# A fused attention and two feed-forwards: the first feed-forward's sums in single PSUM banks, and the split of its result later in the step

## Chip, cores and metric

The kernel runs on 1 core of one Trainium2 chip. The metric is the device time of one execution in microseconds (us), the median of several runs. Engines are named as in the profile: PE is TensorE (PEld its weight loads), DVE is VectorE, ACT is ScalarE, POOL is GpSimd and SP is SyncE, which here only issues DMAs.

## What is computed

The reference chains three blocks. The attention masks its scores by hash buckets of queries and keys. Its output, 1536 tokens of 512 numbers, is the input of feed-forward A, whose output is the input of feed-forward B:

```
h = x @ w_in                                   # A: 512 -> 2048
P = a[0] + a[1]*h + a[2]*h*h + a[3]*h*h*h
Q = 1 + |b[0]|*|h| + |b[1]|*h*h
x2 = (P / (Q + 1e-6)) @ w_out                  # 2048 -> 512

p = sinkhorn(exp(x2 @ w_gate - max))           # B: 1536 tokens, 8 experts, 8 rounds
for e in range(8):
    out += p[:, e:e+1] * (relu(x2 @ w1[e]) @ w2[e])     # 512 -> 1024 -> 512
```

The weights of A arrive as 64-bit floats and are narrowed on the chip; those of B are 32-bit.

## The kernel before

**Products of halves.** Every large operand is split into a high part (fp32r) and a low part (what the high part misses). A product is three matmuls: high by high, high by low, low by high. The tile pairs are `xh`/`xl` for A's input, `gh`/`gl` for hidden activations, `x2h`/`x2l` for B's input, `wa` and `wb` for the weights of a feed-forward's first and second product.

**Feed-forward A in steps.** The hidden width of 2048 is cut into 4 quarters `qf` of 4 blocks of 128, the tokens into 3 tiles `tt` of 512. A pair (qf, tt) is a unit, and a unit has 4 steps, one for each block: 48 steps in all (`NS`), numbered s = 0 to 47 here. PE does in step s:

- `gemm1` (L346, called by `step_a`): 12 matmuls into a bank `h`, called h(s) below;
- `gemm2_a` (L396), from step 6 on: 12 matmuls of the unit that is complete by then, for one of 4 blocks of output rows, into `acca`. It is called g2(s) below. It reads the hidden activations of four earlier steps, the youngest of step s-3.

`acca` is one PSUM tile of two banks, and g2(s) writes bank `j % 2` of it. `sum_a` then adds this bank to the running sum `part` in SBUF (DVE, L407; for the first quarter a copy on ACT, L104 with the output `part`). In the last quarter the finished `part` is split into `x2h` (ACT, L104) and `x2l` (DVE, L107), which B's first product reads.

**Activation.** `activate_a` (L358 to 377) turns h(s) into `gh` and `gl`: ACT forms `tw`, `tq`, `tu` (L364 to 366), POOL a product (L367), DVE two (L368, L369). One step later ACT forms the reciprocal in a bank `tr` (L372 log, L373 exponential), DVE does three operations (L374, L375, L376), ACT writes `gh` (L104) and POOL `gl` (L101). Banks `h` and `tr` come from one set of 4 single banks (tag "b").

**Narrowing the weights.** `prep_weights` works in pieces: ACT takes absolute values (L165), POOL clips (L166), DVE assembles bits in four operations (L176 to L179) over a second two-bank tile `cvt`, POOL adds (L182), ACT writes the high part, POOL the low part. It happens in two of every three steps, from step 3 to step 37.

**What sets the order.** PSUM has 8 banks: 4 single ones under tag "b", and 2 tiles of two banks under tag "s". The latter serve the attention's scores, then `acca` and `cvt`, then B's accumulators `acc0` and `acc1`. In feed-forward A, and in the first 6 steps of B beside it (s = 48 to 53), the order on PE, ACT, DVE and POOL is the order in which the loop over s (L630 to 662) issues the work (`manual_schedule`). On DVE this is, in step s: L374, L375, L376 of step s-1; L368, L369 of step s; the four bit operations if there are any; L407. The lists `old_w`, `acting` and `narrowing` hold work of the step before; `summing` holds the sums whose split into halves is still to come, and `old_s` resumes them, ahead of all the others.

**Feed-forward B.** 8 experts by 3 token tiles by 8 blocks make 192 steps: 12 matmuls of the first product (`step_b`, L346) and 12 of the second (`gemm2_b`, L441), accumulated over the 8 blocks in the four banks of `acc0` and `acc1`. After the last block DVE adds the four banks, weighted, to `osum` (L454). Outside the hand-ordered loop a scheduler sets the order.

Of the kernel before, what the change touches and what calls it, by code (L numbers as in the profile page):

```python
# [13 lines left out]
F32 = mybir.dt.float32  # L14
# [8 lines left out]
PSUM = bass.MemoryType.PSUM  # L23
# [11 lines left out]
def kernel(  # L35
# [22 lines left out]
    P = 128  # L58
# [26 lines left out]
    ps = ctx.enter_context(tc.tile_pool(name="ps", bufs=4, space=PSUM))  # L85
# [2 lines left out]
        return ps.tile([P, 512], F32, tag="b", bufs=4, name=name)  # L88

    def two_banks(name):  # L90
        return ps.tile([P, 2, 512], F32, tag="s", bufs=2, name=name)

    def split(eng_hi, eng_lo, hi, lo, src):
        eng_hi(hi, src)
# [8 lines left out]
    def act_copy(o, src):  # L103
        act.activation(o, src, AF.Copy)  # L104

    def dve_lo(lo, src, hi):
        dve.tensor_tensor(lo, src, hi.bitcast(F32), ALU.subtract)  # L107


    qkv_pool_stack = ExitStack()  # L110
    ap = qkv_pool_stack.enter_context(tc.tile_pool(name="attn", bufs=2))
    heads = [(b, h) for b in range(B) for h in range(H)]
    loaded = {}

# [54 lines left out]
    def narrow_b(bits, c):  # L169


        ci = c.bitcast(I32)
        pc = c if cvt is None else cvt[:, 0]
        pi = pc.bitcast(I32)
        low, high = bits[:, :, 0], bits[:, :, 1]
        dve.tensor_scalar(pi, ci, 5, 2, ALU.logical_shift_left, ALU.logical_shift_right)  # L176
        dve.scalar_tensor_tensor(high, high, -0x40000000, pi, ALU.bitwise_and, ALU.bitwise_or)
        dve.tensor_scalar(pi, high, -0x800000, None, ALU.bitwise_and)  # L178
        dve.scalar_tensor_tensor(low.bitcast(F32), low.bitcast(U32), 2.0 ** -52, pc, ALU.mult, ALU.mult)  # L179
# [4 lines left out]
    def prep_weights(m, i):  # L184

        if i >= NW:
            return
        one = wide and i < NA_W
        c, j = (i, 0) if one else divmod(i - NA_W, 2) if wide else divmod(i, 2)
        if wide and not one:  # L190
            c += NA_W
        r = raws[m, c]
        t = wslots[(i % NSLOT) // 4].tile([P, 2, 512], F32R, tag=f"w{'ab'[m]}{i % NSLOT}", name="w" + "ab"[m])
        slots[m, i] = tuple(t[:, k].rearrange("p (c f) -> p c f", c=KC) if m == 0 else t[:, k] for k in range(2))
        if one:
            bits = (r.rearrange("p c f -> p (c f)") if m == 0 else r[:, 0]).rearrange("p (n t) -> p n t", t=2)
            n = narrow_a(bits)
            yield
            narrow_b(bits, n)
            yield  # L200
            narrow_c(bits, n)
            load_weights(m, c + 2)
            yield
            act_copy(t[:, 0], n)
            yield
            pool_lo(t[:, 1], n, t[:, 0])
            return
        if m == 0:
            split(pool_hi, pool_lo, t[:, 0].rearrange("p (c f) -> p c f", c=KC),
                  t[:, 1].rearrange("p (c f) -> p c f", c=KC), r[:, :, j * P:(j + 1) * P])  # L210
        else:
            split(pool_hi, pool_lo, t[:, 0], t[:, 1], r[:, j])
        if j == 1:
            load_weights(m, c + 2)
# [138 lines left out]


    units = [(qf, tt) for qf in range(NQ) for tt in range(TT)]
    ahid = {}

    def activate_a(hps, gh, gl):  # L358

# [21 lines left out]
    def step_a(n, f):  # L381
        qf, tt = units[n]
        gh, gl = ahid[n, f] = hidden()
        hps = gemm1(slots[0, qf * QF + f], xh[tt], xl[tt])
        return activate_a(hps, gh, gl)

    def gemm2_a(n, j):
        qf, tt = units[n]
        o = acca[:, j % 2]
        js = slice(j * P, (j + 1) * P)  # L390
        m = 0
        for f in range(QF):
            bh, bl = slots[1, qf * QF + f]
            gh, gl = ahid[n, f]
            for l, r in ((bh, gh), (bh, gl), (bl, gh)):
                pe.matmul(o, lhsT=l[:, js], rhs=r, start=m == 0, stop=m == 3 * QF - 1)  # L396
                m += 1

    def sum_a(n, j):

        qf, tt = units[n]
        o = acca[:, j % 2]
        if qf == 0:
            part[tt, j] = sums.tile([P, 512], F32, tag=f"sum{tt}{j}", name="part")
            act_copy(part[tt, j], o)
            return
        dve.tensor_tensor(part[tt, j], part[tt, j], o, ALU.add)  # L407
        if qf == NQ - 1:
            yield
            if j == 0:  # L410
                x2h[tt] = xpool.tile([P, KC, 512], F32R, tag="xh", name="x2h")
                x2l[tt] = xpool.tile([P, KC, 512], F32R, tag="xl", name="x2l")
            act_copy(x2h[tt][:, j], part[tt, j])
            dve_lo(x2l[tt][:, j], part[tt, j], x2h[tt][:, j])
# [3 lines left out]
    bhid, baccs = {}, {}  # L418

    def step_b(n):  # L420
        e, tt, f = steps[n]
        gh, gl = bhid[n] = hidden()
        hps = gemm1(slots[0, FF // P + e * EF + f], x2h[tt], x2l[tt])

        def activate():
            act.activation(gh, hps, AF.Relu)  # L426
            dve.scalar_tensor_tensor(gl, hps, 0.0, gh.bitcast(F32), ALU.max, ALU.subtract)  # L427
        return activate

    def gemm2_b(n):  # L430
        e, tt, f = steps[n]
        bh, bl = slots[1, FF // P + e * EF + f]
        gh, gl = bhid[n]
        if f == 0:
            baccs[tt] = (two_banks("acc0"), two_banks("acc1"))
        acc = baccs[tt]
        for j in range(4):
            o = acc[j // 2][:, j % 2]
            js = slice(j * P, (j + 1) * P)
            for m, (l, r) in enumerate(((gh, bh), (gh, bl), (gl, bh))):  # L440
                pe.matmul(o, lhsT=l[:, js], rhs=r, start=f == 0 and m == 0, stop=f == EF - 1 and m == 2)  # L441
        if f == EF - 1:
            pr = gate["p"]
            for j in range(4):
                o = acc[j // 2][:, j % 2]
                n_ = tt * 4 + j
                if e == 0:
                    osum[n_] = sums.tile([P, 512], F32, tag=f"sum{tt}{j}", name="osum")
                if (e, tt) == (0, 0):
                    act_copy(osum[n_], o)  # L450
                elif e == 0:
                    dve.tensor_scalar(osum[n_], o, pr[:, n_, 0:1], None, ALU.mult)
                else:
                    dve.scalar_tensor_tensor(osum[n_], o, pr[:, n_, e:e + 1], osum[n_], ALU.mult, ALU.add)  # L454
                if e == E - 1:
                    b, c = divmod(n_, C)
                    sp.dma_start(out.rearrange("(b p c) d -> b c p d", b=B, c=C)[b, c], osum[n_])
# [83 lines left out]
    prep_head_b(0)  # L541

    wprep = {NG - 13 + 3 * j: j for j in range(QF)}
    cvt = None
    for it in range(NG + VLAG):
        if it == CONST_AT:
            ca = const.tile([P, 4], F32, name="ca")
# [40 lines left out]
                list(prep_weights(m, wprep[it]))  # L588
    qkv_pool_stack.close()

    def ffn_pool(name, bufs):
        return ctx.enter_context(tc.tile_pool(name=name, bufs=bufs, reuse_waits="tile"))

    wslots[1] = ffn_pool("wslots1", 1)
    mp = ffn_pool("ffn", 2)
    sums = ffn_pool("sums", 1)

    acca, cvt = two_banks("acca"), two_banks("cvt")
    NU, NS, NB_ = len(units), len(units) * QF, len(steps)
    QS = TT * QF  # L600

# [19 lines left out]
    def go(gen):  # L621

        return next(gen, 0) is None
# [3 lines left out]
    narrowing, acting, summing = [], [], []  # L627
    with tc.manual_schedule(engines={mybir.EngineType.PE, mybir.EngineType.Activation, mybir.EngineType.DVE,
                                     mybir.EngineType.Pool}):
        for s in range(NS + QF + ALAG):  # L630
            n = s - NS
            if n < 0:
                new = step_a(*divmod(s, QF))
            else:
                new = step_b(n)
            u, j = divmod(s - ALAG - QF, QF)
            if 0 <= u < NU:
                gemm2_a(u, j)
            old_w = narrowing
            narrowing = [prep_weights(m, i) for m, i in preps.get(s, ())]  # L640
            narrowing = [w for w in narrowing if go(w)]
            old_s = [w for w in summing if go(w)]
            for w in old_w:
                go(w)
            for w in acting:
                go(w)
            if n < 0:
                go(new)
            else:
                new()  # L650
            for w in acting:
                go(w)
            for w in old_w:
                go(w), go(w)
            for w in narrowing:
                go(w)
            summing = []
            if 0 <= u < NU:
                w = sum_a(u, j)
                if go(w):  # L660
                    summing.append(w)
            acting = [new] if n < 0 else []
        assert not (summing and any(go(w) for w in summing)) and not narrowing
# [52 lines left out]
```

## Time and profile before

| | us |
|---|---|
| median of 3 runs | 1665.94 (1664.51 to 1666.65) |
| the profiled execution, its own time | 1664.14 |
| its span, first to last instruction | 1662.4 |
| PE busy | 1591.3 (96%) |
| DVE busy | 736.7 (44%) |
| POOL busy | 657.3 (40%) |
| ACT busy | 563.3 (34%) |

Some 1.7 us of the execution's own time lie outside the span. Busy shares are averages over three stages with different limits: the attention up to about 292 us, feed-forward A up to about 619 us, feed-forward B to the end. The page's 40 slices show it: DVE is busy for seven to nine tenths of each slice up to slice 14 (about 590 us) and for one tenth after it, while PE is at nine or more nearly everywhere.

### The profile page before, as it was taken

The page shows a single profiled execution, that of the slowest core. Times are in us where ns is not written, and L with a number is a line of the kernel's source. Part 1 is how long each engine was busy: PE and PEld are TensorE (multiplying, and loading weights), DVE is VectorE, ACT ScalarE, POOL GpSimd, SP SyncE. Part 2 cuts the span into 40 slices and gives each one's busy share as a digit, 9 for nine tenths or more (in the row PEclk, how much of TensorE's full clock was granted, in tenths as well). Part 3 has the DMA queues.
Part 4 walks back from the last instruction along what each step waited for, and adds up shares of the span by engine and source line. Part 5 has one row for each costly group of instructions (what it writes and reads, how often), then busy time and mean ns, then how long its engine had stood idle before and what let it go on. Part 6 is the DMA issues. An engine that isn't in the chain of part 4 may idle for free.

```text
span 1662.4 us, 19660 instructions
## 1 busy us (share of the span) xinstructions
PE 1591.3 (96%) x7683; PEld 1317.5 (79%) x7683; DVE 736.7 (44%) x1314; ACT 563.3 (34%) x1025; POOL 657.3 (40%) x696
## 2 busy tenths in 40 slices
PE   6999999798888999999999999999999999999998
PEld 5888888576666787888888888888888888888887
DVE  7999999788888742311111111111111111111112
ACT  4887888787676731111111111111111111111110
POOL 7688775677667650150051051042033024015000
PEclk8999999999999999999999999999999999999999
DMA  5232220022111110020020011011012002001001
GB/s 166 80 91 75 73 67 14 26 64 64 51 51 52 38 51 13 14 76 13 1 76 26 0 64 38 1 51 51 1 37 65 0 26 76 1 13 38 1 26 51
DMA packets 49389, 71.67 MB, mean 43 GB/s; under 512 B 4369, under 2 KB 35089, under 8 KB 49297
## 3 DMA queue, kind: packets, MB, share of 16 engines
q1 hardware_dynamic: 49296, 70.42, 14.0%
q8 instruction: 60, 0.98, 0.2%
q14 instruction: 33, 0.26, 0.0%
HBM read 59.79 MB, written 3.15 MB: 38 GB/s over the span
## 4 chain that ended last, share of the span: by engine, by line
PE 74%; DVE 13%; ACT 4%; POOL 4%; issue 3%; DMA 0%; DVEq 0%; POOLq 0%
PE h L346 33%; PE acc L441 31%; PE acca L396 3%; PE av L315 2%; PE pt L300 2%; POOL e L286 1%; DVE tq L374 1%; DVE tu L376 1%; DVE tr L375 1%; DVE e L278 1%; DVE tu L368 1%; DVE ptl L107 1%; DVE cvt L178 1%; DVE cvt L176 1%; DVE part L407 1%
## 5 line engine op out<-in xcount | busy, mean ns | idle before, releaser
L346 PE MATMUL h<-x2h,wa 128*128 128x512 f32 x1536 | 504.7, 390 | 0.0
L427 DVE SCALAR_TENSOR_TENSOR gl<-h,gh 128x512 fp32r<-128x512 f32 x192 | 132.7, 691 | 797.4 <-ACT gh L426 797.4
L441 PE MATMUL acc<-wb,gh 128*128 128x512 f32 x1536 | 474.4, 389 | 0.0
L426 ACT ACTIVATE gh<-h 128x512 fp32r<-128x512 f32 x192 | 114.8, 598 | 894.3 <-PE h L346 894.3
L346 PEld LDWEIGHTS h<-x2h,wa 128*128 128x128 f32 x1536 | 288.5, 188 | 60.1
L441 PEld LDWEIGHTS acc<-wb,gh 128*128 128x128 f32 x1536 | 288.0, 188 | 60.0
L441 PE MATMUL acc<-wb,gl 128*128 128x512 f32 x768 | 298.8, 389 | 0.0
L346 PE MATMUL h<-x2l,wa 128*128 128x512 f32 x768 | 298.8, 389 | 0.0
L98 POOL TENSOR_SCALAR wa<-ra 128x512 fp32r<-128x512 f32 x64 | 40.3, 630 | 533.5 <-PE h L346 533.4
L441 PEld LDWEIGHTS acc<-wb,gl 128*128 128x128 f32 x768 | 144.1, 188 | 29.9
L346 PEld LDWEIGHTS h<-x2l,wa 128*128 128x128 f32 x768 | 144.0, 188 | 29.6
L396 PE MATMUL acca<-gh,wb 128*128 128x512 f32 x384 | 129.8, 399 | 28.9 <-DVE part L407 21.7
L346 PE MATMUL h<-xh,wa 128*128 128x512 f32 x384 | 127.2, 393 | 6.9 <-DVE tu L376 6.9
L396 PEld LDWEIGHTS acca<-gh,wb 128*128 128x128 f32 x384 | 72.2, 188 | 55.2 <-DVE part L407 26.5
L107 DVE TENSOR_TENSOR ptl<-pt,pth 128x512 fp32r<-128x512 f32 x144 | 94.3, 680 | 15.3 <-ACT pth L104 14.5
L286 POOL TENSOR_SCALAR e<-e,rs 128x768 f32<-128x768 f32 x96 | 90.2, 951 | 24.2 <-DVE rs L284 14.6
L279 ACT ACTIVATE e<-e,nm 128x768 f32<-128x768 f32 x96 | 89.8, 935 | 8.5 <-DVE e L278 7.7
L278 DVE TENSOR_SCALAR_CACHE_REDUCE e<-s 128x768 f32<-128x768 f32 x96 | 90.8, 947 | 2.0 <-PE s L271 1.7
L300 PE MATMUL pt<-idr,e 128*128 128x128 f32 x576 | 82.5, 278 | 9.2 <-DVE ptl L107 4.0
L346 PEld LDWEIGHTS h<-xh,wa 128*128 128x128 f32 x384 | 72.5, 189 | 23.6 <-DVE tu L376 8.6
L101 POOL TENSOR_TENSOR wa<-ra,wa 128x512 fp32r<-128x512 f32 x64 | 84.0, 1313 | 5.3
L101 POOL TENSOR_TENSOR wb<-rb,wb 128x512 fp32r<-128x512 f32 x64 | 83.7, 1308 | 5.2
(149 smaller groups left out, 2027.2 us busy)
## 6 DMA issues: line engine op xcount, KB each, us to landing
ra<-in_moe_w_dram SPq DMA_DIRECT2D x32, 512.0 KB
rb<-in_moe_w_dram SPq DMA_DIRECT2D x32, 512.0 KB
ra<-in_moe_w_in_dram SPq DMA_DIRECT2D x16, 512.0 KB
rb<-in_moe_w_out_dram SPq DMA_DIRECT2D x16, 512.0 KB
qkv<-in_q_dram SPq DMA_DIRECT2D x16, 192.0 KB
qkv<-in_k_dram SPq DMA_DIRECT2D x16, 192.0 KB
qkv<-in_v_dram SPq DMA_DIRECT2D x16, 192.0 KB
a<-a SPq DMA_DIRECT2D x16, 192.0 KB
```

The lines of the kernel that those rows point to most:

```text
L98: pool.tensor_scalar(hi, src, 1.0, 0.0, ALU.mult, ALU.add)
L101: pool.tensor_tensor(lo, src, hi.bitcast(F32), ALU.subtract)
L107: dve.tensor_tensor(lo, src, hi.bitcast(F32), ALU.subtract)
L278: dve.tensor_scalar(e[j], s[:, 0:S], BIG, None, ALU.min, ALU.min, accum_out=nm)
L279: act.activation(e[j], e[j], AF.Exp, bias=nm, scale=-1.0, accum_out=rs[:, j:j + 1])
L286: pool.tensor_scalar(e[j], e[j], rs[:, j:j + 1], 0.0, ALU.mult, ALU.add)
L300: pe.transpose(pt[:, c, j * P:(j + 1) * P], e[j][:, cc * P:(cc + 1) * P], idf)
L346: pe.matmul(hps, lhsT=a[:, c], rhs=x[:, c], start=m == 0, stop=m == 3 * KC - 1)
L396: pe.matmul(o, lhsT=l[:, js], rhs=r, start=m == 0, stop=m == 3 * QF - 1)
L426: act.activation(gh, hps, AF.Relu)
L427: dve.scalar_tensor_tensor(gl, hps, 0.0, gh.bitcast(F32), ALU.max, ALU.subtract)
L441: pe.matmul(o, lhsT=l[:, js], rhs=r, start=f == 0 and m == 0, stop=f == EF - 1 and m == 2)
```

## The change

Two things change.

**Banks.** The two-bank tiles stay for the attention alone, in a pool of their own (`ps_s`) that is closed with it. The four banks then go to a pool `ps_f` with single-bank tiles: three in turn under tag "f" and one under tag "c". `gemm2_a` takes a new tile from "f" for each g2(s), which `sum_a` finds under `aacc`. `narrow_b` takes the bank "c" for its bits (named `bits` now). B's four accumulators are the three "f" banks and "c".

**Order.** The second half of `sum_a`, which writes `x2h` and `x2l`, moves from the head of the next step to behind the `gh`, `gl` and weight pieces of that step, ahead of the next sum.

```
@@ two_banks
-        return ps.tile([P, 2, 512], F32, tag="s", bufs=2, name=name)
+        return ps_s.tile([P, 2, 512], F32, tag="s", bufs=2, name=name)
@@ narrow_b
-        pc = c if cvt is None else cvt[:, 0]
+        pc = sum_bank(3, "bits") if bits_in_psum else c
@@ gemm2_a
-        o = acca[:, j % 2]
+        o = sum_bank(0, "acca")
+        aacc[n, j] = o
@@ sum_a
-        o = acca[:, j % 2]
+        o = aacc.pop((n, j))
@@ gemm2_b
-            baccs[tt] = (two_banks("acc0"), two_banks("acc1"))
+            baccs[tt] = [sum_bank(j, f"acc{j}") for j in range(4)]
...
-            o = acc[j // 2][:, j % 2]
+            o = acc[j]
@@ after the attention
-    acca, cvt = two_banks("acca"), two_banks("cvt")
+    ps_f = ffn_pool("ps_f", 1, space=PSUM)
+
+    def sum_bank(j, name):
+
+        return ps_f.tile([P, 512], F32, tag="f" if j < 3 else "c", bufs=3 if j < 3 else 1, name=name)
+
+    bits_in_psum = True
@@ the loop over s
             narrowing = [w for w in narrowing if go(w)]
-            old_s = [w for w in summing if go(w)]
             for w in old_w:
                 go(w)
...
             for w in old_w:
                 go(w), go(w)
+            old_s, summing = summing, []
+            for w in old_s:
+                go(w)
             for w in narrowing:
                 go(w)
-            summing = []
             if 0 <= u < NU:
```

**On PE**, in the second quarter of A. These are one h(s), and the first rows of the g2(s) behind it, with the semaphores that they wait for (DVE_49 counts what DVE has finished); before:

```order
L346 MATMUL h_5190<-xh_97,wa_4304 128x512
L346 MATMUL h_5190<-xl_100,wa_4304 128x512
L346 MATMUL h_5190<-xh_97,wa_4304 128x512 x2
L346 MATMUL h_5190<-xl_100,wa_4304 128x512
L346 MATMUL h_5190<-xh_97,wa_4304 128x512 x2
L346 MATMUL h_5190<-xl_100,wa_4304 128x512
L346 MATMUL h_5190<-xh_97,wa_4304 128x512 x2
L346 MATMUL h_5190<-xl_100,wa_4304 128x512
L346 MATMUL h_5190<-xh_97,wa_4304 128x512
L396 MATMUL acca_4157<-gh_4699,wb_4398 128x512 [waits DVE_49]
L396 MATMUL acca_4157<-gl_4700,wb_4398 128x512
```

The same place with the change (its line numbers are 1 and 2 higher):

```order
L347 MATMUL h_5222<-xh_100,wa_4310 128x512 [waits DVE_49]
L347 MATMUL h_5222<-xl_103,wa_4310 128x512
L347 MATMUL h_5222<-xh_100,wa_4310 128x512 x2
L347 MATMUL h_5222<-xl_103,wa_4310 128x512
L347 MATMUL h_5222<-xh_100,wa_4310 128x512 x2
L347 MATMUL h_5222<-xl_103,wa_4310 128x512
L347 MATMUL h_5222<-xh_100,wa_4310 128x512 x2
L347 MATMUL h_5222<-xl_103,wa_4310 128x512
L347 MATMUL h_5222<-xh_100,wa_4310 128x512
L398 MATMUL acca_5235<-gh_4716,wb_4406 128x512
L398 MATMUL acca_5235<-gl_4717,wb_4406 128x512
```

The matmuls stand in the same order; the wait for DVE has gone from the head of g2(s) to the head of h(s). Before, the operation waited for is L407 on the sum of g2(s-1). With the change it is L376 (L377 there) of step s-3, the last to read the bank that h(s) takes over.

**On DVE**, in the last quarter, the first two steps that finish a `part`; before:

```order
L407 TENSOR_TENSOR part<-part,acca 128x512
L107 TENSOR_TENSOR x2l<-part,x2h 128x512
L374 SCALAR_TENSOR_TENSOR tq<-tq,dbias,tr 128x512
L375 SCALAR_TENSOR_TENSOR tr<-tu,na,tr 128x512
L376 SCALAR_TENSOR_TENSOR tu<-tq,tr 128x512
L368 TENSOR_TENSOR tu<-tu,h 128x512
L369 SCALAR_TENSOR_TENSOR tu<-tu,na,h 128x512
L407 TENSOR_TENSOR part<-part,acca 128x512
L107 TENSOR_TENSOR x2l<-part,x2h 128x512
```

With the change:

```order
L409 TENSOR_TENSOR part<-part,acca 128x512
L375 SCALAR_TENSOR_TENSOR tq<-tq,dbias,tr 128x512
L376 SCALAR_TENSOR_TENSOR tr<-tu,na,tr 128x512
L377 SCALAR_TENSOR_TENSOR tu<-tq,tr 128x512
L369 TENSOR_TENSOR tu<-tu,h 128x512
L370 SCALAR_TENSOR_TENSOR tu<-tu,na,h 128x512
L107 TENSOR_TENSOR x2l<-part,x2h 128x512
L409 TENSOR_TENSOR part<-part,acca 128x512
```

`x2l` has moved behind the five operations of the activation. On ACT `x2h` moves by a whole step in the same way, from behind `gh` of the step before to behind `gh` of this step. The orders on POOL and SP are the same.

## Rows read from the trace of the kernel before

**Rows 1.** Busy time by stage: engines PE, PEld, DVE, ACT, POOL, then PEclk.

```profile
398.00:529.00 131.00, 110.64 (x472) 87.14 (x471) 117.23 (x177) 91.19 (x147) 89.55 (x80) 1.00 0.17 53
529.00:592.00 63.00, 61.67 (x267) 49.52 (x267) 48.98 (x72) 43.31 (x70) 45.40 (x41) 1.00 0.11 34
679.00:1657.00 978.00, 978.00 (x4317) 809.77 (x4316) 185.60 (x271) 107.04 (x179) 217.80 (x228) 1.00 0.10 31
```

**Rows 2.** Waits, 398 to 532 us: total, times, longest.

```profile
PE acca L396 <- DVE part L407: 20.4, 14, 3.0
DVE tq L374 <- ACT tr L373: 8.6, 7, 2.1
DVE tu L368 <- ACT tu L366: 4.5, 6, 0.8
```

**Rows 3.** The chain that ended last, 404 to 430 us: start, us, what.

```profile
410.29 0.69 DVE part L407
...
411.02 3.02 PE acca L396 x12
414.04 2.73 PE h L346 x12
416.79 0.61 ACT tw L364
...
418.94 0.70 DVE tu L368
```

**Rows 4.** Timeline, 404 to 424 us: start, us, engine, operation [idle before <- releaser].

```profile
404.08 0.74 DVE L374 SCALAR_TENSOR_TENSOR tq<-tq,dbias,tr 128x512 f32<-128x512 f32 x1
...
410.88 0.74 DVE L374 SCALAR_TENSOR_TENSOR tq<-tq,dbias,tr 128x512 f32<-128x512 f32 x1
...
415.38 0.58 ACT L373 ACTIVATE tr<-tr 128x512 f32<-128x512 f32 x1
...
416.06 0.75 DVE L374 SCALAR_TENSOR_TENSOR tq<-tq,dbias,tr 128x512 f32<-128x512 f32 x1 [1.07 <-ACT tr L373]
...
417.51 0.69 DVE L376 SCALAR_TENSOR_TENSOR tu<-tq,tr 128x512 f32<-128x512 f32 x1
...
423.70 0.74 DVE L374 SCALAR_TENSOR_TENSOR tq<-tq,dbias,tr 128x512 f32<-128x512 f32 x1
```

**Rows 5.** Timeline, 312 to 317 us.

```profile
313.65 0.74 DVE L374 SCALAR_TENSOR_TENSOR tq<-tq,dbias,tr 128x512 f32<-128x512 f32 x1
...
315.84 0.50 PE L346 MATMUL h<-xh,wa 128*128 128x512 f32 x1 [3.15 <-DVE tu L376]
```

**Rows 6.** Timeline of PE and DVE, 526 to 619 us.

```profile
528.62 0.74 DVE L374 SCALAR_TENSOR_TENSOR tq<-tq,dbias,tr 128x512 f32<-128x512 f32 x1
...
533.23 0.75 DVE L374 SCALAR_TENSOR_TENSOR tq<-tq,dbias,tr 128x512 f32<-128x512 f32 x1 [0.51 <-ACT tr L373]
...
537.07 0.39 PE L346 MATMUL h<-xh,wa 128*128 128x512 f32 x1
...
618.86 0.39 PE L441 MATMUL acc<-wb,gh 128*128 128x512 f32 x1
```

**Rows 7.** Waits, 532 to 619 us.

```profile
ACT x2h L104 <- DVE part L407: 23.3, 12, 3.1
DVE x2l L107 <- ACT x2h L104: 8.4, 12, 0.7
PE acca L396 <- DVE part L407: 1.3, 4, 0.4
```

**Rows 8.** Timeline, 1648 to 1663 us.

```profile
1656.51 2.77 DVE L454 SCALAR_TENSOR_TENSOR osum<-acc,gp,osum 128x512 f32<-128x512 f32 x4 [8.20 <-PE acc L441]
...
1657.44 0.39 PE L441 MATMUL acc<-wb,gl 128*128 128x512 f32 x1
```

**Rows 9.** Busy time in two short stretches, columns as in rows 1.

```profile
316.00:320.00 4.00, 4.00 (x12) 3.15 (x13) 3.86 (x7) 3.94 (x7) 2.69 (x3) 0.64 0.43 133
403.00:406.00 3.00, 1.78 (x8) 1.48 (x9) 2.96 (x5) 0.85 (x2) 2.29 (x2) 1.00 0.04 10
```

More of the change, by code (lines that the diff above doesn't have):

```diff
@@ L111 @@
     ap = qkv_pool_stack.enter_context(tc.tile_pool(name="attn", bufs=2))
+    ps_s = qkv_pool_stack.enter_context(tc.tile_pool(name="ps_s", bufs=2, space=PSUM))
     heads = [(b, h) for b in range(B) for h in range(H)]
@@ L355 @@
     units = [(qf, tt) for qf in range(NQ) for tt in range(TT)]
-    ahid = {}
+    ahid, aacc = {}, {}
     def activate_a(hps, gh, gl):
@@ L444, in gemm2_b @@
             for j in range(4):
-                o = acc[j // 2][:, j % 2]
+                o = acc[j]
                 n_ = tt * 4 + j
@@ L543 @@
     wprep = {NG - 13 + 3 * j: j for j in range(QF)}
-    cvt = None
+    bits_in_psum = False
     for it in range(NG + VLAG):
@@ L589, with ffn_pool @@
     qkv_pool_stack.close()
-    def ffn_pool(name, bufs):
-        return ctx.enter_context(tc.tile_pool(name=name, bufs=bufs, reuse_waits="tile"))
+    def ffn_pool(name, bufs, **kw):
+        return ctx.enter_context(tc.tile_pool(name=name, bufs=bufs, reuse_waits="tile", **kw))
     wslots[1] = ffn_pool("wslots1", 1)
```

## Prediction, made before the changed kernel was run

> **What bounds the kernel now.** I read the busy time by stage first, since the page's averages mix stages. In feed-forward B, PE is busy for all of its 978 us with 4317 matmuls recorded, 0.2265 us each [rows 1]: a group of 12 takes 2.72 us, a step of two groups 5.44, and nothing else can matter there. In feed-forward A between 398 and 529 us PE is busy for 110.6 of 131 us, while DVE has 117.2 [rows 1]. So this stage is where a wait can be removed, and DVE is nearly full in it.
>
> The waits come next. PE waited 14 times, 20.4 us in all, at the head of g2(s) for DVE's sum L407 [rows 2]: g2(s) writes one bank of `acca` while L407 reads the other, and still the first waits for the second, because the two banks are one tile. The same view shows what DVE itself waited for: the exponential L373 (8.6 us in 7 waits) and ACT's `tu` L366 (4.5 us in 6) [rows 2].
>
> The chain of waits and the timeline say which of these waits sets the pace. Let D(s) be the time at which DVE begins step s with L374. From 404.08, 410.88 and 416.06 to 423.70 [rows 4], three steps take 6.80, 5.18 and 7.64 us, 19.62 in all, and this triple repeats through the second and third quarter, as narrowing does; three steps of matmuls alone would be 16.32.
> - The 6.80 step is DVE without a gap: ten operations and a sum behind each other.
> - The 5.18 step has no bits to assemble; DVE ends early and waits 1.07 us for L373 [rows 4]. ACT, fed by DVE's own L376, is the cause, not PE.
> - The 7.64 step is again ten operations, and 0.84 us longer than 6.80. Here the chain leaves DVE: sum L407 at 410.29, g2 at 411.02, h at 414.04, ACT at 416.79, DVE's L368 at 418.94 [rows 3]. PE was held by the sum, h came late, and so DVE waited in turn.
>
> **The change, part by part.** Numbers are for the profiled execution (1664.14 us); the median of the runs, 1665.94, is 1.8 above it.
>
> *The wait of g2(s) goes, and one at h(s) is next.* With three banks in turn, g2(s) needs the sum of g2(s-3) and no longer that of g2(s-1). What is left is the wait of h(s) for L376 of step s-3, which DVE does as its third operation in step s-2. This wait is seen before: D is 313.65, and h starts at 315.84, having waited for L376 [rows 5], 2.19 us after that D. There PE is two steps ahead of DVE, which the sums have prevented from step 7 on. So I take: with the change, while DVE is the slower, h(s) starts at D(s-2) + 2.19.
>
> *Term 1, DVE's own pace.* With PE two steps ahead h(s) is done before ACT asks for it. ACT's exponential ends at 415.96 (415.38 + 0.58 [rows 4]); `tw`, `tq`, `tu` and the start of L368 take 2.15 us (416.79 to 418.94 [rows 3]), so L368 could start at 418.1, and DVE is free for it no sooner (L376 runs from 417.51 to 418.20 [rows 4]). The 7.64 step becomes 6.80, 0.84 saved, 6 times [rows 2]: **5.0 us**. The 1.07 stays, since PE is not in it. Bounds: 0, if ACT is late all the same; 11.5, if both gaps went (6 x 1.91).
>
> The Trainium skill has a measurement that speaks against this part: on the page "TensorE: Matmul & The Clock Gate", section "HAM oscillation — how this bites in real kernels", adding double buffers in PSUM to a matmul kernel gave no further gain. By that the time would stay at 1664.1. In this case's trace the wait for the bank is on the chain itself, for 0.84 us in every third step, and that decides for me.
>
> *Term 2, PE's lead when the narrowing ends.* Step 37 is the last with bits. After it DVE's steps are shorter than PE's 5.44, and PE alone sets the time; what it has done by then is won. Before, D(38) is 528.62 and h(40) starts at 537.07, 8.45 later [rows 6]. With the change h(40) starts at D(38) + 2.19, with PE there in time: h(39) may start at D(37) + 2.19 = D(38) - 4.61, and a step later is D(38) + 0.83, plus 0.15 for a start after a wait (g2 and h of rows 3 end 5.75 us after 411.02, where two groups and the overhang of the last matmul would be 5.60). Saved: 8.45 - 2.19 = **6.3 us**. The next h(41) needs D(39) + 2.19; D(39) comes 4.61 after D(38) [rows 6], so the limit is D(38) + 6.80, and PE comes at 7.8. From there PE doesn't wait. Bounds: 0, if the lead is eaten further on; 8.5, if h(40) started with D(38).
>
> *Term 3, the last quarter.* From h(40) at 537.07 to B's first group at 618.86 [rows 6] are 81.79 us for 29 groups (78.88) and one matmul of B that stood early (0.23): 2.7 lost. It went in four waits for sums, 1.3 us [rows 7], in restarts, and in late steps of the halves: ACT stood with `x2h` at the head of its step, 12 times for 23.3 us, and DVE behind it with `x2l` [rows 7]. Now `x2h` stands behind `gh`, a step after its sum. The costs that it is moved past: on ACT the five operations of a step wait no longer; on DVE the five of the activation come first, then `x2l`, then the next sum; POOL and SP keep their order, and no DMA moves. `x2h` of token tile 0 is complete in step 46 instead of at its head, and h(48) is the first to read it: PE has g2(46), h(47) and g2(47) between, 8.2 us, which covers the move of a few us; without that cover the delay would land on h(48) once. DVE's sum for such a step, 4.1 (the 5.18 less its gap of 1.07 [rows 4]) plus some 0.7 for `x2l`, stays below 5.44. Saved: 2.7 less one restart, **2.5 us**. Bounds: -4 (one late h(48)) to 2.7.
>
> *Term 4, the end.* The last four `osum` start at 1656.51 with the first pair of banks and run back to back for 2.77 us, while the last matmul ends 0.39 after 1657.44 [rows 8]. By single banks the first can start 0.69 earlier, and the last starts with the last matmul's end, at 1657.9 instead of 1658.5: **0.7 us**. Bounds 0 and 0.7.
>
> *At nothing.* B's accumulators as four tiles: the matmuls and their order stay, and PE has no gap there [rows 1]. The bits' bank: same DVE operations on PSUM in the same order. The first quarter of A: its sums are copies on ACT, and DVE's steps there wait only for ACT; PE will wait at h instead of g2.
>
> Sum: 5.0 + 6.3 + 2.5 + 0.7 = 14.5, of which the bounds make anything from 0 to 23. 1664.1 - 14.5 = 1649.6 for an execution like the profiled one, and **1651.4** at the level of the median.
>
> **The rivals.**
> - *The lead is given back* (13%). Something in the last quarter (late `x2h`, weights of B not yet there when PE comes 13 us sooner) holds PE once; terms 2 and 3 go, 5.0 + 0.7 stay: 1660.2. For it: ACT's `x2h` is a step later, and rows 7 show that ACT's place in the queue was a price. Against: 8.2 us of cover.
> - *More than that* (7%). The 1.07 us gaps go too, 6.4 us: 1645.0. For it: ACT's queue shifts when its `tw` comes earlier. Against: the gap begins with DVE's L376 and runs over ACT alone.
> - *It does not do what it says* (5%): if the wait at h(s) bites as the one at g2(s) did, the same chain closes over PE and 0 to 2 us come out: 1664 to 1666. Against: L376 of step s-3 is done long before the sum of s-1.
> - *Slower, by the clock* (5%). One gap of 3.15 us [rows 5] was followed by a granted clock of 0.64 between 316 and 320 us [rows 9], that is, the lower of the levels 1.2 and 2.4 GHz for most of it: 12 matmuls took 4.0 us [rows 9] where 2.72 is usual, 1.3 us lost. A gap of 3.0 [rows 2] was not followed by one (1.00 [rows 9]). If the waits at h, some 22 of them (two in three steps from 8 to 40), brought such a fall each, 29 us would be lost: 1680. It is slower from 12 falls on. Against: my waits are at most 1.2 us long (6.80 less 5.44 and a restart), shorter than the longest now.
>
> The Trainium skill names this rival: "TensorE: Matmul & The Clock Gate", section "A second HAM failure mode: psum-queue depth-cycling", tells of a kernel that cycled through PSUM banks and in which short idle times of TensorE let its clock swing. The granted clock of 1.00 from 398 to 529 us, with 14 waits in it, does not show that.
>
> **How the numbers follow.** 70% for my forecast, 1651.4, by itself 1649 to 1654 (a fall of the clock more or less, and the spread of 2 us of the runs). The range takes in most of the rival that gives the lead back, and a part of the faster one: 1647 to 1659. 0.2% is 3.3 us, about what a measurement of this kernel can tell from no change. Faster by more: 70 + 13 + 7 = 90%; within it 5%; slower 5%.
>
> **What would show it.** Right: no wait of g2 for L407; waits of h for DVE in A, at most 1.2 us each after step 7; DVE's triple 18.8 instead of 19.6; PE without a gap from about 526 us to B, whose first group starts near 605; B as long as before. Wrong: a triple of 19.6 (term 1), a gap of PE between 526 and 605 (terms 2 and 3), a granted clock under 1 after 330 us, or PE gaps at B's token tiles.

## The result, and the profile after

The changed kernel took 1649.84 us (median of 4 runs, 1649.72 to 1650.8) against 1665.37 for the kernel before, measured beside it: a ratio of 0.9906, with a 95% interval from 0.9894 to 0.9919. 1651.4 had been predicted, in a range from 1647 to 1659. The profiled execution took 1650.80 us with a span of 1649.0; before it was 1664.14 and 1662.4.

Stage by stage (columns as in rows 1; the last stretch is as long as that of rows 1 and lies 13 us earlier):

```profile
398.00:529.00 131.00, 117.69 (x501) 92.58 (x500) 121.17 (x182) 94.09 (x154) 92.89 (x85) 1.00 0.18 57
529.00:592.00 63.00, 63.00 (x280) 52.17 (x279) 52.83 (x73) 42.42 (x69) 50.85 (x45) 1.00 0.16 51
666.00:1644.00 978.00, 978.00 (x4316) 809.90 (x4315) 183.44 (x273) 107.22 (x179) 217.94 (x228) 1.00 0.10 31
```

Feed-forward B is what it was. Between 398 and 529 us PE did 501 matmuls instead of 472, and between 529 and 592 it has no gap left. The waits of 398 to 532 us, as in rows 2:

```profile
PE h L347 <- DVE tu L377: 13.3, 14, 1.1
...
DVE tq L375 <- ACT tr L374: 9.1, 8, 2.1
```

No wait of g2 for a sum is left; PE waits as often as before, but at the head of h and for at most 1.1 us, and DVE no longer waits for ACT's `tu`. In the last quarter (532 to 606 us, in the same view) PE waits for nothing, and the 12 waits of `x2h` [rows 7] have become 2:

```profile
ACT x2h L104 <- DVE part L409: 3.1, 2, 2.3
```

The timeline of one triple, with the starts of DVE's steps (L375), the waits of h, and what ACT does in the step without bits:

```profile
430.80 0.74 DVE L375 SCALAR_TENSOR_TENSOR tq<-tq,dbias,tr 128x512 f32<-128x512 f32 x1
...
432.96 0.63 ACT L104 ACTIVATE gh<-tu 128x512 fp32r<-128x512 f32 x1 [2.44 <-DVE tu L377]
...
432.98 0.50 PE L347 MATMUL h<-xh,wa 128*128 128x512 f32 x1 [1.07 <-DVE tu L377]
...
433.50 0.62 ACT L104 ACTIVATE wa<-c 128x512 fp32r<-128x512 f32 x1
...
434.02 0.67 ACT L166 ACTIVATE c<-rb 128x512 f32<-128x512 f32 x1
...
434.59 0.68 ACT L373 ACTIVATE tr<-tq,dbias 128x512 f32<-128x512 f32 x1
...
435.30 0.58 ACT L374 ACTIVATE tr<-tr 128x512 f32<-128x512 f32 x1
...
435.98 0.75 DVE L375 SCALAR_TENSOR_TENSOR tq<-tq,dbias,tr 128x512 f32<-128x512 f32 x1 [1.08 <-ACT tr L374]
...
442.80 0.74 DVE L375 SCALAR_TENSOR_TENSOR tq<-tq,dbias,tr 128x512 f32<-128x512 f32 x1
...
444.98 0.50 PE L347 MATMUL h<-xh,wa 128*128 128x512 f32 x1 [0.80 <-DVE tu L377]
...
449.60 0.74 DVE L375 SCALAR_TENSOR_TENSOR tq<-tq,dbias,tr 128x512 f32<-128x512 f32 x1
```

From 430.80 to 449.60 are 18.80 us: steps of 5.18, 6.82 and 6.80. The step of 7.64 [rows 4] is gone, the gap of 1.07 at the end of the short one is still there. h starts 2.18 us after a step of DVE begins, at 432.98 and 444.98 alike. The end of narrowing and the first group of B, in the same view:

```profile
524.79 0.74 DVE L375 SCALAR_TENSOR_TENSOR tq<-tq,dbias,tr 128x512 f32<-128x512 f32 x1
...
526.98 0.50 PE L347 MATMUL h<-xh,wa 128*128 128x512 f32 x1 [1.07 <-DVE tu L377]
...
606.02 0.62 PE L443 MATMUL acc<-wb,gh 128*128 128x512 f32 x2
```

These are D(38), h(40) and B's start; before they are in rows 6. With D(1), the first step of DVE in feed-forward A, the whole difference can be split:

| us | before | after | difference | predicted |
|---|---|---|---|---|
| span's start to D(1) | 298.69 | 299.76 | +1.07 | 0 |
| D(1) to D(38) | 229.93 | 225.03 | -4.90 | -5.0 (term 1) |
| D(38) to h(40) | 8.45 | 2.19 | -6.26 | -6.3 (term 2) |
| h(40) to B's first group | 81.79 | 79.04 | -2.75 | -2.5 (term 3) |
| from there to the end | 1043.51 | 1043.01 | -0.50 | -0.7 (term 4) |
| span | 1662.37 | 1649.02 | -13.34 | -14.5 |

The tail behind the last row, in the timeline:

```profile
1643.21 2.79 DVE L456 SCALAR_TENSOR_TENSOR osum<-acc,gp,osum 128x512 f32<-128x512 f32 x4 [7.52 <-PE acc L443]
...
1644.83 0.39 PE L443 MATMUL acc<-wb,gl 128*128 128x512 f32 x1
```

The four sums end 0.78 us after the last matmul (1646.00 less 1645.22), and 1.45 after it before the change [rows 8].

The first row of the table can't be put down to the change. Over the eleven kernels traced here, one execution each and with the same attention, D(1) lies anywhere from 297.61 to 300.18: on the old banks from 298.69 to 300.03, on the new ones over the whole range. Distances below are therefore taken from D(1).

### The profile page after: what moved, and what is told of

It is laid out like the page before. It is cut to its first block, busy times and chain, and to the rows that moved or that the text cites. A ratio compares the mean times of both kernels' runs of the same rounds, so it can differ in the third digit from the quotient of the medians.

```text
span 1649.0 us, 19659 instructions
## 1 busy us (share of the span) xinstructions
PE 1590.8 (96%) x7683; PEld 1318.4 (80%) x7683; DVE 734.2 (45%) x1314; ACT 561.7 (34%) x1025; POOL 657.5 (40%) x696
## 4 chain that ended last, share of the span: by engine, by line
PE 75%; DVE 12%; POOL 4%; ACT 3%; issue 3%; DMA 0%; POOLq 0%; DVEq 0%
PE h L347 34%; PE acc L443 32%; PE av L316 3%; PE acca L398 3%; PE pt L301 2%; DVE tq L375 2%; DVE tu L377 2%; POOL e L287 2%; DVE tr L376 2%; DVE bits L179 1%; DVE bits L177 1%; DVE ptl L107 1%; DVE e L279 1%; DVE tu L369 1%; PE s L271 1%
## 5 line engine op out<-in xcount | busy, mean ns | idle before, releaser
L347 PE MATMUL h<-xh,wa 128*128 128x512 f32 x384 | 130.7, 402 | 23.4 <-DVE tu L377 23.4
L398 PE MATMUL acca<-gh,wb 128*128 128x512 f32 x384 | 126.0, 389 | 0.0
L107 DVE TENSOR_TENSOR ptl<-pt,pth 128x512 fp32r<-128x512 f32 x144 | 94.3, 681 | 15.8 <-ACT pth L104 15.0
L98 POOL TENSOR_SCALAR wb<-rb 128x512 fp32r<-128x512 f32 x64 | 40.8, 638 | 110.3 <-PE acc L443 97.2
```

The costliest lines, as they stand in the source:

```text
L98: pool.tensor_scalar(hi, src, 1.0, 0.0, ALU.mult, ALU.add)
L347: pe.matmul(hps, lhsT=a[:, c], rhs=x[:, c], start=m == 0, stop=m == 3 * KC - 1)
```

## The experiments

The theory was that of the prediction: the bank in turn takes the sum off PE's path, DVE's own pace is left, and PE's lead when narrowing ends is won. The rivals were the other half of the change (the halves' place), the need for a third bank, and a pace that is not DVE's. Each kernel is compared with the kernel before, measured beside it. Line numbers shift by a few from kernel to kernel.

### The banks without the move, and the move without the banks

```
@@ the loop over s (on the changed kernel)
+            old_s = [w for w in summing if go(w)]
             for w in old_w:
...
-            old_s, summing = summing, []
-            for w in old_s:
-                go(w)
             for w in narrowing:
                 go(w)
+            summing = []
```

> The single banks as in the change, the halves x2h and x2l at their old place at the head of the next step. Theory of the prediction: the banks bring terms 1, 2 and 4, and of the 2.7 us of term 3 the 1.3 us that were waits for sums; what is left to the halves is at most 1.4 us. So 1649.8 to 1651.3, a triple of 18.8 us in narrowing, PE at h(40) within 0.2 us of where the change has it, and B's first group in acc 79.0 to 80.5 us after h(40). Rival: with PE ahead of DVE, it is the late place of the halves that keeps ACT free for tw and so PE fed in the last quarter; then steps of 6.07 us, as DVE has them there before the change, come back 12 times and PE is held by them: 1654 to 1657.

Measured: 1650.08 us, ratio 0.9911 (0.9897 to 0.9925). From h(40) to B's first group it is 79.26 us, 0.2 more than with the move. ACT stands with `x2h` as often as before the change, DVE waits 0.57 us for ACT in each step, and its steps have the 6.07 us of the rival (waits of 532 to 606 us; timeline):

```profile
ACT x2h L104 <- DVE part L409: 20.5, 12, 2.8
```

```profile
555.17 0.75 DVE L375 SCALAR_TENSOR_TENSOR tq<-tq,dbias,tr 128x512 f32<-128x512 f32 x1 [0.57 <-ACT tr L374]
...
561.25 0.75 DVE L375 SCALAR_TENSOR_TENSOR tq<-tq,dbias,tr 128x512 f32<-128x512 f32 x1 [0.57 <-ACT tr L374]
```

PE is held there only once, and late, at h(49), by a load of weights (timeline):

```profile
575.59 0.19 PEld L347 LDWEIGHTS h<-x2h,wa 128*128 128x128 f32 x1 [0.29 <-DVE tu L377]
```

It costs PE the 0.2 us. DVE enters these steps ahead, after four of 4.1 to 5.6 us, and loses 0.63 in each of the six to PE's 5.44; that just uses up what it had. PE is not held step by step, and the rival falls, though with few such steps to spare. With the banks in place, then, the move is worth 0.2 us.

The other half, on the kernel before:

```
@@ the loop over s (on the kernel before)
-            old_s = [w for w in summing if go(w)]
...
+            old_s, summing = summing, []
+            for w in old_s:
+                go(w)
             for w in narrowing:
                 go(w)
-            summing = []
```

> The kernel before with only the halves moved behind gh, gl and the weight pieces. Theory of the prediction: no part of terms 1 and 2, so the triple stays 19.6 us and h(40) 8.4 us behind D(38); of term 3 at most the late halves, up to 1.4 us: 1663.9 to 1665.4. Rival: the move carries a good part of the gain, because ACT no longer stands with x2h at the head of its step: 1658 or less.

Measured: 1662.91 us, ratio 0.9989 (0.9981 to 0.9998), 1 us below the expected range and far from the rival. Up to the end of narrowing nothing has moved: D(38) is 230.19 after D(1), and h(40) comes 8.43 after it, behind the old wait (timeline).

```profile
529.69 0.74 DVE L374 SCALAR_TENSOR_TENSOR tq<-tq,dbias,tr 128x512 f32<-128x512 f32 x1
...
529.83 0.50 PE L396 MATMUL acca<-gh,wb 128*128 128x512 f32 x1 [1.06 <-DVE part L407]
...
538.12 0.39 PE L346 MATMUL h<-xh,wa 128*128 128x512 f32 x1
```

From h(40) to B it is 79.92 us instead of 81.79. So by the traces the move alone is worth 1.9 us in the last quarter, the banks alone 2.5, and both 2.75: the expectation had added up what overlaps. The move frees ACT where PE has no lead; where PE has one, it frees nobody that is waited for.

### Two banks in turn

```
-        return ps_f.tile([P, 512], F32, tag="f" if j < 3 else "c", bufs=3 if j < 3 else 1, name=name)
+        return ps_f.tile([P, 512], F32, tag="f" if j < 2 else "c", bufs=2, name=name)
```

> The change with two banks in turn for the sums and two for the bits (B's accumulators use all four). Theory of the prediction: what matters is that g2(s) no longer waits for the sum of g2(s-1); with two banks it waits for that of s-2, which DVE ends as step s-1 begins, so g2(s) starts at D(s-1) at the earliest and h(s+1) at D(s-1) + 2.87 instead of + 2.19. DVE's pace is not touched: triple 18.8 us, waits of g2 for the sum up to 1.2 us in place of those of h, h(40) 0.7 us later: 1650.5, between 1649.8 and 1651.5. Rival: three banks are needed, since two were there before and PE waited; then the triple is 19.6 us and the time 1660 to 1665.

Measured: 1651.56 us, ratio 0.9921 (0.9907 to 0.9934), just above the expected 1651.5. The waits are back at g2, and cost DVE nothing (timeline: D(38), the wait of g2(39) behind it, h(40)):

```profile
525.07 0.74 DVE L375 SCALAR_TENSOR_TENSOR tq<-tq,dbias,tr 128x512 f32<-128x512 f32 x1
...
525.21 0.50 PE L398 MATMUL acca<-gh,wb 128*128 128x512 f32 x1 [1.06 <-DVE part L409]
...
528.06 0.39 PE L347 MATMUL h<-xh,wa 128*128 128x512 f32 x1
```

A g2(s) that waits starts 0.14 us after D(s-1), the triple is 18.8, and h(40) comes 2.99 after D(38) instead of 2.19. From D(1) to h(40) it is 0.66 us more than with three banks, where 0.7 was expected. There were two banks before, too; what held PE was that they were one tile, so that one bank's sum was waited for by a product that writes the other.

### Whose pace it is: an operation less

```
-        dve.tensor_scalar(pi, high, -0x800000, None, ALU.bitwise_and)
+        if not bits_in_psum:
+            dve.tensor_scalar(pi, high, -0x800000, None, ALU.bitwise_and)
```

> The change without the third of the four bit operations in feed-forward A (the one that masks sign and exponent, 0.695 us on DVE in each step with bits; the low parts of A's weights come out otherwise). Theory of the prediction: DVE alone sets the pace of the 6.80 steps, so each loses 0.69 us and the triple becomes 17.4 us; the gap of 1.07 us in the step without bits stays. Six triples: 8.3 us, and about as much again for each of the four triples of the first quarter (6.21 us steps): up to 5 us more, 1637 to 1642. Rival: the pace is that of the loop over ACT and POOL, in which DVE's operations stand by chance without gaps: a gap of 0.69 us opens in front of L375 or L369 and the time stays at 1649 to 1650.

Measured: 1630.06 us, ratio 0.9788 (0.9775 to 0.9801): below the expected range, and far from the rival. The gap of 1.07 stays, and the steps with bits take 5.95 instead of 6.80 (timeline):

```profile
435.56 0.74 DVE L376 SCALAR_TENSOR_TENSOR tq<-tq,dbias,tr 128x512 f32<-128x512 f32 x1
...
440.74 0.75 DVE L376 SCALAR_TENSOR_TENSOR tq<-tq,dbias,tr 128x512 f32<-128x512 f32 x1 [1.07 <-ACT tr L375]
...
446.69 0.74 DVE L376 SCALAR_TENSOR_TENSOR tq<-tq,dbias,tr 128x512 f32<-128x512 f32 x1
```

So DVE is the pace of these steps, as the theory says, but the expectation priced the operation wrongly. It is busy for 0.69 us and cost 0.85, in each of 24 steps: 20.4 us, against 20.7 found between D(1) and B's start. The first quarter, put at up to 5 us, gave 9.5 of it.

### The gap of 1.07 us

```
@@ the loop over s
-            narrowing = [prep_weights(m, i) for m, i in preps.get(s, ())]
-            narrowing = [w for w in narrowing if go(w)]
             for w in old_w:
                 go(w)
...
                 new()
+            narrowing = [prep_weights(m, i) for m, i in preps.get(s, ())]
+            narrowing = [w for w in narrowing if go(w)]
+            for w in old_w:
+                go(w)
             for w in acting:
                 go(w)
             for w in old_w:
-                go(w), go(w)
+                go(w)
```

> The change with ACT's absolute value of the next piece and its copy of the finished one taken out from between gh and the logarithm: both now stand behind tu and ahead of gh, where ACT waits for DVE anyway. Theory (the gap of 1.07 us in the step without bits is ACT's chain from L377: gh 0.63, copy 0.62, absolute value 0.67, logarithm 0.68, exponential 0.58): the chain becomes 1.89 us, shorter than the 2.05 us that DVE has to do meanwhile, and the gap closes to 0.1 or so. Triple 17.8 us instead of 18.8 in the second and third quarter (6 times 1.0) and up to 1.3 us less in each of some five triples of the first, where the gap is 2.1 us: 1637 to 1643. Rival: the gap is PE's after all, or moves to POOL's clip in front of L177: 1648 to 1650.

Measured: 1640.25 us, ratio 0.9853 (0.984 to 0.9866). The chain of ACT, and DVE's steps (timeline):

```profile
422.93 0.74 DVE L375 SCALAR_TENSOR_TENSOR tq<-tq,dbias,tr 128x512 f32<-128x512 f32 x1
...
425.09 0.63 ACT L104 ACTIVATE gh<-tu 128x512 fp32r<-128x512 f32 x1 [0.83 <-DVE tu L377]
...
425.62 0.68 ACT L373 ACTIVATE tr<-tq,dbias 128x512 f32<-128x512 f32 x1
...
426.33 0.58 ACT L374 ACTIVATE tr<-tr 128x512 f32<-128x512 f32 x1
...
427.01 0.75 DVE L375 SCALAR_TENSOR_TENSOR tq<-tq,dbias,tr 128x512 f32<-128x512 f32 x1
```

The logarithm follows `gh` at once, the step without bits takes 4.08 us without a gap, and the triple is 17.81. From D(1) to D(19) the kernel gains 5.3 us on the changed one, from D(19) to D(37) 5.9. The gap was ACT's order, as the prediction read it.

### The last pieces of narrowing later

```
-            prep_at(qf * QS + (6, 7, 12, 13)[j], 1, (qf + 1) * QF + j)
+            prep_at(qf * QS + (6, 7, 12, 13)[j] + 2 * (qf == NQ - 2 and j >= 2), 1, (qf + 1) * QF + j)
```

> The change with the last two pieces of narrowing two steps later (steps 38 and 39 instead of 36 and 37). Theory of term 2 (what PE has done when the narrowing ends is won, and PE's 5.44 us per step hides DVE's slower steps only as far as its lead goes): D(38) comes 5.4 us earlier, h(40) starts at D(38) + 2.19 as before, and h(41), h(42) wait again, 1.4 us each, for two steps of 6.80: 5.4 less 2.7, so 2.7 us are gained, 1647.1, between 1645.5 and 1648.5. Rival: only the number of DVE's operations up to B counts, not when they come: 1649.8. Second rival: g2(42) reads the weights of these pieces, and comes too soon for them: slower than 1650.

Measured: 1647.59 us, ratio 0.9896 (0.9883 to 0.991); from D(1) to B's first group 2.6 us less than with the change. The value is the expected one, the way to it is not (timeline: D(35) and h(37), then D(40) and h(42)):

```profile
503.74 0.74 DVE L375 SCALAR_TENSOR_TENSOR tq<-tq,dbias,tr 128x512 f32<-128x512 f32 x1
...
505.93 0.50 PE L347 MATMUL h<-xh,wa 128*128 128x512 f32 x1 [1.04 <-DVE tu L377]
...
530.72 0.74 DVE L375 SCALAR_TENSOR_TENSOR tq<-tq,dbias,tr 128x512 f32<-128x512 f32 x1
...
533.28 0.39 PE L347 MATMUL h<-xh,wa 128*128 128x512 f32 x1
```

The last wait of PE is that of h(37), 2.19 us after D(35). From there PE runs at 5.44 us a step; DVE's two steps without bits put it ahead of PE, so h(41) and h(42) find their bank free (533.28 against D(40) + 2.19 = 532.91). From h(37) on PE alone sets the time, with two pieces of narrowing still to come: a lead hides them, as the theory says. That DVE's later pieces cost 2.7 of the 5.4 us through waits was wrong: PE was the later one there.

### The bits between other operations

```
@@ the loop over s (narrow_b yields behind each operation, activate_a behind L369 and L376)
-            for w in acting:
+            for w in acting + narrowing + acting + narrowing:
                 go(w)
...
+            for w in narrowing + [new] * (n < 0) + narrowing:
+                go(w)
...
-            for w in narrowing:
-                go(w)
```

> The change with DVE's four bit operations of a step placed one each between the five of the activation, so that an operation no longer stands right behind the one whose result it reads. Leaving out one of the four took 0.85 us from a step, not the 0.69 that it is busy: operations that read the one before start 0.72 to 0.79 us apart, the others 0.60 to 0.66. Theory (DVE sets the pace, dependencies included): a step of 6.80 becomes 6.2, one of 6.21 becomes 5.7, 24 times 0.55: some 13 us, 1635 to 1639, with the gap of 1.07 still there. Rival: the spacing goes with the kind of operation and not with the dependence: no change, 1649 to 1650. Second rival: L377 comes 0.6 us later, so gh and the release of h's bank do, and ACT's chain takes it all back: 1645 to 1655.

Measured: 1634.02 us, ratio 0.9815 (0.9802 to 0.9829), 15.8 less than the median of the change, with the same operations, and 1 us below the expected range. Two of the bit operations behind each other in the changed kernel, from its timeline; the second reads what the first writes:

```profile
440.14 0.69 DVE L178 SCALAR_TENSOR_TENSOR rb<-rb,bits 128x512 int32<-128x512 int32 x1
440.86 0.69 DVE L179 TENSOR_SCALAR bits<-rb 128x512 int32<-128x512 int32 x1
```

They start 0.72 us apart. A step of DVE with bits in the new order, from its timeline:

```profile
431.97 0.74 DVE L379 SCALAR_TENSOR_TENSOR tq<-tq,dbias,tr 128x512 f32<-128x512 f32 x1
432.62 0.75 DVE L380 SCALAR_TENSOR_TENSOR tr<-tu,na,tr 128x512 f32<-128x512 f32 x1
433.28 0.69 DVE L177 TENSOR_SCALAR bits<-c 128x512 int32<-128x512 int32 x1
433.88 0.68 DVE L382 SCALAR_TENSOR_TENSOR tu<-tq,tr 128x512 f32<-128x512 f32 x1
434.47 0.68 DVE L179 SCALAR_TENSOR_TENSOR rb<-rb,bits 128x512 int32<-128x512 int32 x1
...
438.12 0.74 DVE L379 SCALAR_TENSOR_TENSOR tq<-tq,dbias,tr 128x512 f32<-128x512 f32 x1
```

`bits` is written at 433.28 and read at 434.47; between them stands L382, and L382 and L179 each start 0.60 us after the one ahead, though that is busy for 0.69 or 0.68. The step takes 6.15 us instead of 6.80, and 24 times 0.65 are 15.6 us; from D(1) to B's first group it is 15.5 less. The operations are of the same kinds as before, so the rival that the kind sets the spacing falls. On the page "VectorE: DVE Perf Modes", section "The DRAIN you can't avoid", the Trainium skill says that the next operation starts only when the pipe has emptied, and that leaving out the waits between operations gained nothing (it adds that one that isn't held starts earlier). By its first sentence this order would be worth nothing. In this case's traces it is the exception in brackets that holds, with L382 0.60 us behind an operation of 0.69, and the order of the same ten operations is worth as much as the whole change.

### All three, and all three on the old banks

The first of the two has the three edits above together, and the absolute value of a piece a step earlier; the second is the same on the kernel before, with the halves at their new place, so that the two differ in the banks alone.

```
@@ the loop over s (besides the three diffs above)
-            narrowing = [prep_weights(m, i) for m, i in preps.get(s, ())]
-            narrowing = [w for w in narrowing if go(w)]
+            narrowing = coming
+            for m, i in preps.get(s, ()):
+                if i >= NA_W:
+                    go(prep_weights(m, i))
...
+            coming = [prep_weights(m, i) for m, i in preps.get(s + 1, ()) if i < NA_W]
+            coming = [w for w in coming if go(w)]
             for w in old_w:
```

> The three edits together; the absolute value of a piece stands a step earlier, so that its bits can begin behind L376. If each gain holds beside the others (13 and 9 and up to 2.7 us), DVE comes under PE's 16.32 us per triple and PE bounds feed-forward A nearly alone: all waits of h behind step 7 (17.6 us) go, and with a shorter step 6 perhaps the fall of the clock near 316 us: 1626 to 1632. Rival: ACT and POOL, full by then, close the loop before PE does: 1634 to 1640.

Measured: 1625.78 us, ratio 0.9764 (0.9751 to 0.9777), the fastest version here and 0.2 us below the expected range. The fall of the clock near 316 us, which the expectation hoped to lose, is still there (a granted clock of 0.72 from 316 to 320 us). PE has no gap between 398 and 529 us (columns as in rows 1), and DVE's triple, 16.4 us, has come down to PE's 16.32:

```profile
398.00:529.00 131.00, 131.00 (x580) 108.51 (x579) 125.99 (x198) 107.28 (x173) 106.55 (x95) 1.00 0.20 61
```

> The three edits of all_three (and the halves at their new place), but on the two-bank tiles of the kernel before: what are the banks worth when DVE is no longer far behind PE? Theory of terms 1 and 2: g2(s) has to wait for the sum of g2(s-1), so it starts with D(s) and h(s+1) with D(s) + 2.87; that h ends at D(s) + 5.74 and its tu is there at about D(s) + 7.9, while DVE, in the step of 4.09 without bits, wants it at D(s) + 5.5. So PE and DVE hold each other once in three steps, for 2.4 us: a triple of 18.8 instead of 16.4, and h(40) behind D(38) by some 8 us again. Twelve triples at up to 2.4, less what PE's own 5.44 takes of it, and some 3 to 6 us of lead: 1645 to 1655, so the banks are worth 20 to 29 us here. Rival: the banks are worth the same 15 us as in the change, whatever DVE's pace: 1640 to 1642. Second rival: with DVE at PE's pace there is nothing to wait for, and the banks are worth under 5 us: 1626 to 1631.

Measured: 1637.73 us, ratio 0.9829 (0.9816 to 0.9843): by the medians the banks are worth some 12 us here, between the two rivals and below the theory. The timeline of a triple (the first two starts of DVE's steps in it and the next one's first) and PE's waits of 398 to 590 us:

```profile
434.63 0.73 DVE L378 SCALAR_TENSOR_TENSOR tq<-tq,dbias,tr 128x512 f32<-128x512 f32 x1
...
439.43 0.75 DVE L378 SCALAR_TENSOR_TENSOR tq<-tq,dbias,tr 128x512 f32<-128x512 f32 x1 [0.70 <-ACT tr L377]
...
451.92 0.74 DVE L378 SCALAR_TENSOR_TENSOR tq<-tq,dbias,tr 128x512 f32<-128x512 f32 x1
```

```profile
PE acca L401 <- DVE part L412: 2.7, 7, 0.4
```

The triple is 17.29 us and not 18.8: the step without bits is late by 0.7, for ACT's exponential, where 2.4 was expected for ACT's `tu`. The place was right (the one wait of PE in three steps, and the short step as the one that pays); the operation that DVE then waits for, and the size, were not. Of the 12.4 us between the two traces 1.4 lie ahead of D(1), where the attention ends sooner or later from trace to trace, so some 11 are the banks'. From there it is 0.6 up to D(19), 6.5 up to D(37) (5.4 of it six triples of 0.9), 1.3 up to h(40), 1.8 up to B's first group and 0.8 behind it. A lost lead, of which some 3 to 6 us were expected, is not among them: h(40) comes 9.14 us after D(38) on the old banks and 8.91 on the new ones, where PE is busy without a gap and has no lead to lose.

## Why the prediction was right

**Term 1** (5.0) came out as 4.9. The wait of g2 was on DVE's own chain, through h, `tw` and `tu`, in one step of three, and 0.84 us per triple is what a bank in turn could take from it. `two_in_turn` and `no_exponent_mask` show that PE is out of it: waits of PE at another place don't move the triple of 18.8, an operation less on DVE does. What is left beside DVE's own operations is the gap of 1.07, and `copies_earlier` shows that it is ACT's. (The prediction's "ten operations and a sum" of a step are ten with the sum; no number hangs on it.)

**Term 2** (6.3) came out as 6.26; h(40) starts at D(38) + 2.19 to the hundredth. That the release of the bank of h is the next limit of the lead is the step on which this rested, and it was read from one earlier place [rows 5]. `order_alone` keeps the old distance, 8.43.

**Term 3** (2.5) came out as 2.75. Of this 0.23 is the matmul of B that stood early before the change, at 591.43 us, and now stands behind 606.02; without it the term is 2.5. Here the sum was right where the shares were not: the prediction counted the waits for sums, restarts and late halves as parts that add up. Each half of the change removes most of it by itself, the banks 2.5 and the move 1.9, and the move adds 0.2 to the banks.

**Term 4** (0.7) came out as 0.67 at the tail. In the table it is 0.50, since the same matmul of B has come into that row.

**At nothing.** From D(1) to D(19) the first quarter takes 105.39 us before and 105.43 after. B took as long, without a gap.

**The rivals.** The lead was not given back; the gap of 1.07 stayed; the waits at h cost DVE nothing, with a triple of 18.80; the clock did not fall behind any of the 14 waits between 398 and 532 us, where it is 1.00. The Trainium skill's measurement that double buffers in PSUM gave no further gain (page "TensorE: Matmul & The Clock Gate", section "HAM oscillation — how this bites in real kernels", named in the prediction) doesn't carry over to a kernel whose chain holds the wait. With two banks in turn the gain is 13.7 us here, and with three 15.5.

The four terms together came to 14.4 us of the 14.5 predicted; the traces differ by 13.3, because D(1) is 1.07 later in the one of the change. The predicted time was 1.6 us above the measured median, within the spread of D(1). One thing in the prediction doesn't fit together: its range up to 1659 was said to take in most of the rival that gives the lead back, but leaves out the 1660.2 at which that rival was put.

## What to carry to other kernels

Two banks in one tile are one buffer to whoever waits by tiles: before adding buffers, look whether a producer waits for the reader of a part that it doesn't write. Price a removed wait by the chain that it closes (0.84 us of each 19.6 here, not the 20.4 us that the list of waits shows), and add the lead that the fast engine has when the slow stage ends. On an engine that sets the pace, look at the starts of its operations and not at their busy time: two dependent ones in a row cost more than the same two with another between.

## What was not expected of the hardware

**DVE's operations overlap when they don't depend on each other.** In the changed kernel those that read what the one before wrote start 0.72 to 0.79 us apart, others 0.60 to 0.67, and each is busy for 0.68 to 0.75: a busy share of DVE near its full time hides that there is something to gain.

**The lower clock came behind some gaps and not behind others.** At the start of feed-forward A, PE waits four times at the head of h for DVE (L376 in the kernel before). Busy time in short stretches behind the longest of these gaps; of the change, whose gap was 3.19 us (316.91 its end):

```profile
316.00:320.00 4.00, 3.09 (x7) 2.48 (x8) 3.86 (x7) 3.05 (x6) 3.63 (x3) 0.57 0.45 133
```

of `no_exponent_mask`, whose longest gap was 2.31 us (315.79 its end):

```profile
316.00:320.00 4.00, 4.00 (x18) 3.27 (x18) 3.93 (x7) 3.94 (x7) 3.55 (x4) 1.00 0.42 132
```

and of `bits_between`, where the longest gap, 2.10 us, ended at 309.89:

```profile
311.00:313.00 2.00, 2.00 (x7) 1.52 (x6) 2.00 (x5) 1.94 (x5) 1.45 (x2) 0.50 0.00 0
```

A granted clock of 0.50 is the lower level, 1.2 GHz. In `bits_between` the gaps were 1.06, 1.06, 2.10 and 0.94 us, from 300 to 316 us, and the clock fell behind the third. In `no_exponent_mask` they were 1.07, 1.08, 1.62 and 2.31, and it did not fall. The gap of 3.0 at 404 us [rows 2] stood alone and was followed by 1.00 [rows 9]. A rule for when it falls can't be read from these rows.
